# Inverse softmax sums carried to the attention outputs: through DRAM as rows instead of widened copies and TensorE transposes

## The chip, the cores and the metric

The kernel runs on one core of a Trainium2 chip. Its time is the device time of one execution in microseconds (us). Before the change it is 1243.0 us, the median of three runs (1238.74, 1243.0 and 1247.97).

The core has five instruction streams that run beside each other, each in its own order: TensorE (PE, whose weight loads are shown as PEld), VectorE (DVE), ScalarE (ACT), GpSimd (POOL) and the queue that issues the DMAs (SP). Semaphores tie them together.

## The reference

A forgetting attention over 8 batches of 8 heads (576 positions, 64 numbers each), and behind it a feed-forward network over all 4608 tokens, in float32:

```python
scores = scale * np.matmul(q, k.transpose(0, 1, 3, 2))
decay = cum[:, :, :, None] - cum[:, :, None, :]      # cum: running sum of log f
scores = np.where(causal, -1000000000.0, scores + decay)
scores = scores - np.max(scores, axis=-1, keepdims=True)
attn = np.exp(scores)
attn = attn / (np.sum(attn, axis=-1, keepdims=True) + 1e-09)
x = np.matmul(attn, v)                               # heads side by side: 4608 x 512
h = x @ w_in                                         # 512 -> 2048
out = np.maximum(0.01 * h, h) @ w_out                # 2048 -> 512
```

## The kernel before

Every large product is made of three products of rounded parts (`_h` is the high part of a number, `_l` the low part), which is why the feed-forward network, lines L508 and L541, has most of TensorE's matmuls.

**Stages.** First an early stage (to about 160 us): the first 256 positions of batches 0, 1 and 2, and the splitting of the weights. Then 64 tasks, one for each head, in the order of `ORDER` (batches 0, 3, 4, 5, 6, 7, 1, 2). A head of batches 0 to 2 has three chunks of positions left (2, 3 and 4: 320 positions, the last chunk 64 wide), a head of the others five (0 to 4: 576 positions). Last comes what is left of the feed-forward network.

**One iteration** `t` of the loop over tasks works on two heads at once: for each chunk `i` it transposes the probabilities of head `t - 1` (`transposes`, PSUM tiles `tr`, copied out by ACT as `ph` and by DVE as `pl`), and computes the scores of head `t` (`scores`, PSUM tiles `sc`, a masked minimum on DVE, and the exponential on ACT, which also adds up the row sums into `fixed["sum.."]`). Then it computes the outputs of head `t - 1` (`values`, PSUM tiles `av`). Between these pieces `fill(step)` puts portions of the feed-forward network: `h_` tiles (L508), and `o_` tiles (L541), which need `gh` (DVE, L518) and `gl` (POOL, L520).

**Where the sums go.** The outputs of two heads share one tile `x`, with positions as columns and the two heads' 64 numbers as partitions (0 to 63 and 64 to 127). The sums have positions as partitions: `fixed["sum.."]` is 128 x 5 chunks x 2 heads. Once for each pair of heads, in the iteration behind the second head, `inverse` takes the reciprocal (L440, L441) and has POOL repeat each value 64 times into `rw` (L448). `normalise` transposes `rw` on TensorE chunk by chunk into the PSUM tile `rb` (L459), so that each position's factor stands in its column on all 64 partitions of its head; DVE multiplies `x` with it (L460), and the product goes to `xd` in DRAM (L464), from where the feed-forward network fetches it as `xs` (L475).

**What sets the order.** The program is written with a framework that reorders each engine's instructions by its own estimates and gives out buffers by tag. The PSUM tag `tr` has two buffers, which `tr`, `av` and `rb` share, so a tile waits until the last but one before it has been read. The SBUF tags `part0` and `part1`, which hold `rw`, have one buffer each. All DMAs are issued by SP, one after the other: an issue that waits holds up all behind it.

Of the kernel before, what the change touches and what calls it, by code (L numbers as in the profile page):

```python
# [8 lines left out]
F32 = mybir.dt.float32  # L9
# [4 lines left out]
ALU = mybir.AluOpType  # L14

P = 128
# [20 lines left out]
def forgetting_attention_ffn(ctx, tc, qT, kT, v4, vr, f, w_in, w_out, out):  # L37
# [6 lines left out]
    nc = tc.nc  # L44
    NHEAD, D, S = qT.shape
# [4 lines left out]
    NFULL = S // P  # L50
    REST = S - NFULL * P
    NCH = NFULL + 1
# [11 lines left out]
    tasks = [  # L64
        (b * HPB + x, T // P if b < NE else 0, NCH) for b in batches for x in range(HPB)
    ]

    def rows(i):
        return P if i < NFULL else REST

    def width(i):
        return i * P + rows(i)
# [18 lines left out]
    one = ctx.enter_context(tc.tile_pool(name="one", bufs=1))  # L91
    dram = ctx.enter_context(tc.tile_pool(name="dram", bufs=1, space=bass.MemoryType.DRAM))
    psum = ctx.enter_context(tc.tile_pool(name="psum", bufs=2, space=bass.MemoryType.PSUM))
# [18 lines left out]
    ident = ident_r.bitcast(F32)  # L112
# [6 lines left out]
    )  # L119

    xd = dram.tile([DM, NTOK], F32, name="xd")
    dec_k, dec_q = (dram.tile([NHEAD, 2, S], F32, name=n) for n in ("dec_k", "dec_q"))

    fr = one.tile([2 * NHEAD, S], F32, tag="z4", name="fr")
# [59 lines left out]
    for i, r in enumerate(decay_r):  # L184
        n = width(i)
        d = one.tile([P, n], F32, tag=f"z{i}", name=f"d_{i}")
# [4 lines left out]
    for i in range(NCH):  # L191
        c = slice(i * P, width(i))
# [3 lines left out]
    for name, tag, x, to in (("fck", "s1", fc, dec_k), ("fcq", "m1", start, dec_q)):  # L196
        r = one.tile([P, S], F32R, tag=tag, name=name, bufs=2)
# [5 lines left out]
    pairs = {}  # L203

    def load(t):

        s, c0, c1 = tasks[t]
        h = state[t] = {}
        a, n = c0 * P, width(c1 - 1)
        for name, src, lo in (("q", qT, a), ("k", kT, 0)):  # L210
            x = h[name] = one.tile([P, S], F32, tag=f"{name}raw", name=f"{name}raw_{t}")
            for o in range(2):
                nc.sync.dma_start(x[o * D:(o + 1) * D, lo:n], src[s][:, lo:n])
        if s % 2 == 0:
            g = s // 2
            vm = fixed["vm"]
            nc.sync.dma_start(vm[:, :, :NFULL], v4[g])
            nc.sync.dma_start(vm[:REST, :, NFULL], vr[g])
            pairs[s // 2, c0] = {}
# [79 lines left out]
    fixed = {}  # L299
# [38 lines left out]
    def scores(t, i):  # L338

        s, c0, c1 = tasks[t]  # L340
        h = state[t]
        m, n = rows(i), width(i)
        if i < NFULL:
            z = h[f"z{i}"] = one.tile([P, n], F32, tag=f"z{i}", name=f"z{i}_{t}")
        else:
            z = h[f"z{i}"] = fixed["z4"]
        z = z[:m, :n]
        if i == c0:
            h["max"] = one.tile([P, NCH + 1], F32, tag="max", name=f"max_{t}", bufs=3)
        parts = [(0, n)] if n <= 512 else [(0, n // 2), (n // 2, n)]  # L350
        for x, (a, b) in enumerate(parts):
            ps = psum.tile([P, 512], F32, tag="sc", name=f"sc_{t}_{i}_{x}")
            cols = slice(i * P, i * P + m)
            for y, w in enumerate("12"):
                nc.tensor.matmul(  # L355
                    ps[:m, :b - a], h["s" + w][:, cols], h["m" + w][:, a:b],
                    start=y == 0, stop=y == 1,
                )
            at = TRI - P - i * P + a
            nc.vector.tensor_tensor_reduce(  # L360
                out=z[:, a:b], in0=ps[:m, :b - a], in1=tri[:m, at:at + b - a], scale=-SCALE,
                scalar=3.0e38 if x == 0 else h["max"][:m, i:i + 1],
                op0=ALU.add, op1=ALU.min, accum_out=h["max"][:m, i + x:i + x + 1],
            )
        last = i + len(parts) - 1
        nc.scalar.activation(  # L366
            z, z, AF.Exp, bias=h["max"][:m, last:last + 1], scale=-1.0,
            accum_out=fixed["sum" + "ab"[s // 2 % 2]][:m, i, s % 2:s % 2 + 1],
        )

    def transposes(t, i):
        h = state[t]
        if i == tasks[t][1]:
            for w in ("ph", "pl"):
                h[w] = one.tile([P, PTW], F32R, tag=w, name=f"{w}_{t}")
        m = rows(i)
        z = h[f"z{i}"]
        ps = psum.tile([P, 512], F32, tag="tr", name=f"tr_{t}_{i}")

        blocks_ = [NFULL, *range(NFULL)] if i == NFULL else range(i + 1)  # L380
        for x, j in enumerate(blocks_):
            nc.tensor.transpose(  # L382
                ps[:, x * m:(x + 1) * m], z[:m, j * P:(j + 1) * P], ident[:m, :m]
            )
        nblk = len(blocks_)
        for dst, eng in ((h["ph"], "a"), (h["pl"], "v")):
            if nblk == 1:
                o, hi, src = dst[:, PT0:], h["ph"][:, PT0:], ps[:, :m]
            else:
                first = 0 if i == NFULL else place_p(0, i * P)  # L390
                o = strided(dst, first, nblk, PST, m)
                hi = strided(h["ph"], first, nblk, PST, m)
                src = ps[:, :nblk * m].rearrange("p (j m) -> p j m", m=m)
            if eng == "a":
                nc.scalar.copy(o, src)  # L395
            else:
                nc.vector.tensor_tensor(o, src, hi.bitcast(F32), op=ALU.subtract)  # L397
# [37 lines left out]

    def inverse(t):

        s, c0, c1 = tasks[t]
        r = one.tile([P, NCH, 2], F32, tag="r", name=f"r_{t}")
        nc.vector.tensor_scalar(r, fixed["sum" + "ab"[s // 2 % 2]], 1.0e-9, None, op0=ALU.add)  # L440
        nc.vector.reciprocal(r, r)  # L441
        wide = pairs[s // 2, c0]["r"] = {}
        for lo, hi in spans(t):
            c = (hi - lo + P - 1) // P
            w = one.tile([P, c, 2, D], F32, tag=f"part{lo == 0:d}", name=f"rw_{t}_{lo}")
            a = r[:, lo // P:lo // P + c]
            a = bass.AP(tensor=a.tensor, offset=a.offset, ap=[*a.ap, [0, D]])
            nc.gpsimd.tensor_copy(w, a)  # L448
            wide[lo] = w.rearrange("p c o d -> p c (o d)")

    def normalise(t):

        s, c0, c1 = tasks[t]
        pair = pairs[s // 2, c0]
        x, r = pair["x"], pair["r"]
        for part, (lo, hi) in enumerate(spans(t)):
            ps = psum.tile([P, 512], F32, tag="tr", name=f"rb_{t}_{part}")
            for c in range(lo, hi, P):
                nc.tensor.transpose(ps[:, c - lo:c - lo + P], r[lo][:, (c - lo) // P], ident)  # L459
            nc.vector.tensor_tensor(x[:, lo:hi], x[:, lo:hi], ps[:, :hi - lo], op=ALU.mult)  # L460
        b, hp = s // HPB, (s % HPB) // 2
        a, n = c0 * P, width(c1 - 1)
        at = place[b, a]
        nc.sync.dma_start(xd[hp * P:(hp + 1) * P, at:at + n - a], x[:, a:n])  # L464

    def spans(t):
        a, n = tasks[t][1] * P, width(tasks[t][2] - 1)
        return [(a, n)] if n - a <= 512 else [(a + P, n), (a, a + P)]
# [96 lines left out]
    def fill(n):  # L565

        credit[0] += n
        while credit[0] >= 1:
            credit[0] -= 1
            if not next(quanta, None):  # L570
                credit[0] = 0
                return
            used[0] += 1
# [32 lines left out]
    for t in range(nt + 1):  # L606
        heads[0] = t < nt
        if t + 1 < nt:
            load(t + 1)
        before = list(range(*tasks[t - 1][1:])) if t else []  # L610
        now = list(range(*tasks[t][1:])) if t < nt else []
        have = ready[0] // T * NQ - used[0]
        left = min((e + 2 - t for e in ends if e + 1 >= t), default=1)
        step = min(have / (left + SLACK), MAXQ) / 8
        fill(step)
        for i in range(5):
            if i in before:
                transposes(t - 1, i)
            if i in now:
                scores(t, i)  # L620
            fill(step)
        if t:
            for part in range(len(spans(t - 1))):
                if part == 0 and tasks[t - 1][0] % 2:
                    inverse(t - 1)
                values(t - 1, part)
                fill(step)
            if tasks[t - 1][0] % 2:
                normalise(t - 1)
            s, c0, c1 = tasks[t - 1]  # L630
            if s % HPB == HPB - 1:
                ready[0] = place[s // HPB, c0 * P] + width(c1 - 1) - c0 * P
        if t + 1 < nt:
            split(t + 1)
        fill(step * (3 - len(spans(t - 1)) if t else 1))
# [35 lines left out]
```

## Time and profile before

| | |
|---|---|
| median of three runs | 1243.0 us |
| the profiled execution | 1237.03 us, of it 1235.3 us from the first to the last instruction |
| PE busy | 1219.8 us (99%) |
| PEld, ACT, DVE, POOL busy | 1077.1, 635.2, 609.6, 444.0 us |
| granted TensorE clock | 1.00 |
| DMA | 102.47 MB, 27.3% of the 16 engines' span |

Busy time is the time in which an engine had an instruction of the program under way. PE's matmuls overlap each other, so the sum of their durations is more than the busy time, and what one of them costs is better read from the distance between ends. In the profile's rows `out<-in` are tiles by the program's names; a row of the grouped view has the count behind an x, the busy time in us, the mean duration in ns, and the engine's idle time just before these instructions with what ended it. In rows in order of time the first two numbers are the start and the time taken, in us.

### The profile page before, as it was taken

Reading aid. Unit: us, or ns where it says so; the run is one execution under the profiler, and the core shown is the slowest. Engines: PE = TensorE matmul, PEld = TensorE weight load, DVE = VectorE, ACT = ScalarE, POOL = GpSimd, SP = SyncE. Lnnn points to the kernel's source line nnn. Section 1 sums busy time; section 2 is a strip of 40 time slices with the busy share of each in tenths; the row PEclk is TensorE's granted clock in tenths of the full one; section 3 lists DMA queues with packets and bytes.
Section 4 is the critical chain, followed back from the end, with each engine's and each line's share of the span. In section 5 each row is a group of like instructions: output and inputs, shape, how many; then the busy total and the mean of one; then the engine's idle time right before and its main releaser. Section 6 shows DMA issues by size and latency. Waiting matters only on the chain.

```text
span 1235.3 us, 21918 instructions
## 1 busy us (share of the span) xinstructions
PE 1219.8 (99%) x7980; PEld 1077.1 (87%) x7980; DVE 609.6 (49%) x1598; ACT 635.2 (51%) x1511; POOL 444.0 (36%) x395
## 2 busy tenths in 40 slices
PE   9999999999999999999999999999999999999998
PEld 6777788888888989899899999999999998889997
DVE  6888975665554444444434434344343334443211
ACT  6775646667755565555544545454444444651111
POOL 2000254555444344543444443443344334432000
PEclk9999999999999999999999999999999999999999
DMA  6453433343232223322221222221222222211000
GB/s 195 149 168 134 140 100 101 91 119 111 80 113 67 69 84 86 99 69 86 78 86 49 79 69 80 66 77 46 74 73 68 64 61 80 57 53 40 18 18 18
DMA packets 70219, 102.47 MB, mean 83 GB/s; under 512 B 13152, under 2 KB 42384, under 8 KB 70112
## 3 DMA queue, kind: packets, MB, share of 16 engines
q1 hardware_dynamic: 70112, 101.08, 27.3%
q8 instruction: 63, 1.03, 0.4%
q14 instruction: 44, 0.36, 0.1%
HBM read 74.76 MB, written 18.42 MB: 75 GB/s over the span
## 4 chain that ended last, share of the span: by engine, by line
PE 84%; DMA 5%; issue 3%; DVE 3%; ACT 2%; POOL 2%; SPq 1%; POOLq 0%; ACTq 0%; DVEq 0%
PE h L508 29%; PE o L541 29%; PE sc L355 8%; PE av L424 7%; PE tr L382 6%; DMA xs<-xd 2%; PE sce L246 1%; PE rb L459 1%; PE ave L288 1%; DMA xd<-x 1%; DMA kraw<-in_kT 1%; PE sce L249 1%; ACT wt L150 1%; PE warm L105 1%; POOL s L129 1%
## 5 line engine op out<-in xcount | busy, mean ns | idle before, releaser
L508 PE MATMUL h<-xh,win_h 128*128 128x256 f32 x1152 | 331.2, 288 | 0.1
L508 PE MATMUL h<-xh,win_l 128*128 128x256 f32 x1152 | 326.0, 283 | 0.0
L508 PE MATMUL h<-xs,win_h 128*128 128x256 f32 x1024 | 289.2, 282 | 0.0
L520 POOL TENSOR_TENSOR gl<-g,gh 128x512 fp32r<-128x512 f32 x111 | 143.0, 1289 | 307.8 <-DVE gh L518 307.7
L541 PE MATMUL o<-wout_h,gh 128*128 128x512 f32 x576 | 231.0, 402 | 1.5 <-DVE gh L518 1.5
L541 PE MATMUL o<-wout_l,gh 128*128 128x512 f32 x576 | 226.0, 393 | 0.1
L541 PE MATMUL o<-wout_h,gl 128*128 128x512 f32 x576 | 224.8, 392 | 0.7 <-DVE gl L520 0.7
L508 PEld LDWEIGHTS h<-xh,win_h 128*128 128x128 f32 x1152 | 219.4, 191 | 4.4 <-ACT win_h L155 0.5
L508 PEld LDWEIGHTS h<-xh,win_l 128*128 128x128 f32 x1152 | 219.5, 190 | 0.9 <-issue 0.7
L515 ACT ACTIVATE g<-h 128x512 f32<-128x512 f32 x144 | 85.9, 597 | 229.2 <-PE h L508 220.8
L508 PEld LDWEIGHTS h<-xs,win_h 128*128 128x128 f32 x1024 | 195.1, 191 | 3.0
L395 ACT CAST ph<-tr 128x256 fp32r<-128x256 f32 (+3 forms) x272 | 119.5, 445 | 143.2 <-PE tr L382 141.8
L360 DVE CUSTOM_DVE_ANT_0 z<-sc,tri 128x128 f32<-128x128 f32 (+1 forms) x208 | 107.4, 518 | 166.1 <-PE sc L355 166.1
L518 DVE CAST gh<-g 128x512 fp32r<-128x512 f32 x144 | 76.6, 532 | 181.8 <-ACT g L515 179.0
L366 ACT ACTIVATE z<-z,max 128x128 f32<-128x128 f32 (+1 forms) x208 | 122.7, 590 | 79.8 <-DVE max L360 78.7
L397 DVE TENSOR_TENSOR pl<-tr,ph 128x256 fp32r<-128x256 f32 (+3 forms) x272 | 136.7, 508 | 41.4 <-ACT ph L395 41.2
L129 POOL TENSOR_TENSOR s<-qraw,s 64x576 fp32r<-64x576 f32 (+1 forms) x64 | 79.4, 1240 | 182.2 <-ACT s L326 164.5
L541 PEld LDWEIGHTS o<-wout_h,gl 128*128 128x128 f32 x576 | 108.1, 188 | 24.7 <-DVE gl L520 1.2
L355 PE MATMUL sc<-m,s 128*64 128x288 f32 (+1 forms) x336 | 123.2, 372 | 1.8 <-DVE max L360 1.8
L541 PEld LDWEIGHTS o<-wout_h,gh 128*128 128x128 f32 x576 | 108.4, 189 | 18.0 <-DVE gh L518 1.7
L541 PEld LDWEIGHTS o<-wout_l,gh 128*128 128x128 f32 x576 | 108.5, 189 | 16.3 <-issue 0.3
L382 PE MATMUL tr<-ident_r,z 128*128 128x128 f32 x568 | 96.1, 273 | 1.7 <-DVE pl L397 1.1
(112 smaller groups left out, 1807.8 us busy)
## 6 DMA issues: line engine op xcount, KB each, us to landing
kraw<-in_kT SPq DMA_DIRECT2D x128, 144.0 KB
qraw<-in_qT SPq DMA_DIRECT2D x80, 144.0 KB
wraw<-in_w_in SPq DMA_DIRECT2D x16, 512.0 KB
wraw<-in_w_out SPq DMA_DIRECT2D x16, 512.0 KB
fixed_vm<-in_v SPq DMA_DIRECT2D x32, 256.0 KB
xs<-xd SPq DMA_DIRECT2D x16, 512.0 KB
out<-ost SPq DMA_DIRECT2D x28, 256.0 KB
xd<-x SPq DMA_DIRECT2D x20, 288.0 KB
```

The lines of the kernel that those rows point to most:

```text
L129: nc.gpsimd.tensor_tensor(out, a, b, op=ALU.subtract)
L355: nc.tensor.matmul(ps[:m, :b - a], h["s" + w][:, cols], h["m" + w][:, a:b], start=y == 0, stop=y == 1,)
L360: nc.vector.tensor_tensor_reduce(out=z[:, a:b], in0=ps[:m, :b - a], in1=tri[:m, at:at + b - a], scale=-SCALE, scalar=3.0e38 if x == 0 else ...
L366: nc.scalar.activation(z, z, AF.Exp, bias=h["max"][:m, last:last + 1], scale=-1.0, accum_out=fixed["sum" + "ab"[s // 2 % 2]][:m, i, s % 2: ...
L382: nc.tensor.transpose(ps[:, x * m:(x + 1) * m], z[:m, j * P:(j + 1) * P], ident[:m, :m])
L395: nc.scalar.copy(o, src)
L397: nc.vector.tensor_tensor(o, src, hi.bitcast(F32), op=ALU.subtract)
L424: nc.tensor.matmul(ps[:, a - lo:hi - lo], fixed["vs"][:, odd, j, :], h[w][:, at:at + hi - a], start=(n == 0), stop=(n == len(steps) - 1),)
L508: nc.tensor.matmul(ph[:, e, :], w[:, c, fs], xx[:, c, :], start=(c == 0 and x == 0), stop=(c == NCC - 1 and x == 2),)
L515: nc.scalar.activation(g, ph, AF.Prelu, alpha=0.01)
L520: eng.tensor_tensor(gl, g, gh.bitcast(F32), op=ALU.subtract)
L541: nc.tensor.matmul(acc[k], gg[:, e, ts], w[:, e, :], start=(fc_ == 2 * p0 and x == 0), stop=(fc_ == 2 * p1 - 1 and x == 2),)
```

## The change

`inverse` no longer widens on POOL. The reciprocals are laid out with the two heads outermost (10 columns), transposed by one TensorE instruction into 10 rows of 128, copied out by ACT into the unused half of the tile `rest`, and written to a small DRAM tile by one DMA. Four DMAs read them back, each value row repeated over the 64 partitions of its head: two into `main` (the full chunks) and two into `rest` (the last 64 positions). `normalise` loses its transposes; DVE multiplies `x` with `main` and `rest`, which lie in SBUF. The call of `inverse` moves from ahead of `values` to behind chunk 1 of the same iteration.

```diff
+    rows_d = [dram.tile([2, NCH * P], F32, name=f"rows_{x}") for x in range(4)]
...
     def inverse(t):
         s, c0, c1 = tasks[t]
-        r = one.tile([P, NCH, 2], F32, tag="r", name=f"r_{t}")
-        nc.vector.tensor_scalar(r, fixed["sum" + "ab"[s // 2 % 2]], 1.0e-9, None, op0=ALU.add)
+        r = one.tile([P, 2, NCH], F32, tag="r", name=f"r_{t}")
+        sums = fixed["sum" + "ab"[s // 2 % 2]].rearrange("p c o -> p o c")
+        nc.vector.tensor_scalar(r, sums, 1.0e-9, None, op0=ALU.add)
         nc.vector.reciprocal(r, r)
-        wide = pairs[s // 2, c0]["r"] = {}
-        for lo, hi in spans(t):
-            c = (hi - lo + P - 1) // P
-            w = one.tile([P, c, 2, D], F32, tag=f"part{lo == 0:d}", name=f"rw_{t}_{lo}")
-            a = r[:, lo // P:lo // P + c]
-            a = bass.AP(tensor=a.tensor, offset=a.offset, ap=[*a.ap, [0, D]])
-            nc.gpsimd.tensor_copy(w, a)
-            wide[lo] = w.rearrange("p c o d -> p c (o d)")
+        ps = psum.tile([P, 512], F32, tag="tr", name=f"rt_{t}")
+        nc.tensor.transpose(ps[:2 * NCH, :P], r.rearrange("p o c -> p (o c)"), ident)
+        main = one.tile([P, NFULL * P], F32, tag="part0", name=f"rb_{t}")
+        rest = one.tile([P, 2 * P], F32, tag="part1", name=f"rbr_{t}")
+        flat = rest[:2 * NCH, P:]
+        nc.scalar.copy(flat, ps[:2 * NCH, :P])
+        to = rows_d[s // 2 % 4]
+        nc.sync.dma_start(to.rearrange("o (c q) -> (o c) q", q=P), flat)
+        for y, lo, hi in ((main[:, c0 * P:], c0 * P, NFULL * P), (rest[:, :REST], NFULL * P, S)):
+            for o in range(2):
+                nc.sync.dma_start(
+                    y[o * D:(o + 1) * D], to[o:o + 1, lo:hi].broadcast_to([D, hi - lo])
+                )
+        pairs[s // 2, c0]["r"] = main, rest
     def normalise(t):
...
-        for part, (lo, hi) in enumerate(spans(t)):
-            ps = psum.tile([P, 512], F32, tag="tr", name=f"rb_{t}_{part}")
-            for c in range(lo, hi, P):
-                nc.tensor.transpose(ps[:, c - lo:c - lo + P], r[lo][:, (c - lo) // P], ident)
-            nc.vector.tensor_tensor(x[:, lo:hi], x[:, lo:hi], ps[:, :hi - lo], op=ALU.mult)
+        for y, lo, hi in ((main[:, c0 * P:], c0 * P, NFULL * P), (rest[:, :REST], NFULL * P, S)):
+            nc.vector.tensor_tensor(x[:, lo:hi], x[:, lo:hi], y, op=ALU.mult)
...
             if i in now:
                 scores(t, i)
+            if i == 1 and t and tasks[t - 1][0] % 2:
+                inverse(t - 1)
             fill(step)
...
-                if part == 0 and tasks[t - 1][0] % 2:
-                    inverse(t - 1)
                 values(t - 1, part)
```

How the instructions stand now is read from the built programs; the changed program's line numbers are higher by one above `inverse` and by six at the end, and the last number in a name only tells tiles apart. TensorE first, at the pair of heads 18 and 19, the sixth pair with all five chunks (about 393 us). Before, chunk 1 of head 19 is transposed (`tr_1`), chunk 1 of head 20 scored (`sc_1`), and chunk 2 follows at once:

```order
L382 MATMUL tr_1_4717<-ident_r,z_19_4532 128x128 x2
L355 MATMUL sc_1_0_4723<-m_20_4663,s_20_4662 128x256
L355 MATMUL sc_1_0_4723<-fixed_m2a,fixed_s2a 128x256
L382 MATMUL tr_2_4728<-ident_r,z_19_4562 128x128 x3
L355 MATMUL sc_2_0_4735<-m_20_4663,s_20_4662 128x384
L355 MATMUL sc_2_0_4735<-fixed_m2a,fixed_s2a 128x384
```

Now the transpose of the inverses (`rt`) stands there:

```order
L383 MATMUL tr_1_4736<-ident_r,z_19_4551 128x128
L356 MATMUL sc_1_0_4742<-m_20_4682,s_20_4681 128x256
L356 MATMUL sc_1_0_4742<-fixed_m2a,fixed_s2a 128x256
L446 MATMUL rt_4750<-ident_r,r_4747 10x128
L356 MATMUL sc_2_0_4767<-m_20_4682,s_20_4681 128x384
L356 MATMUL sc_2_0_4767<-fixed_m2a,fixed_s2a 128x384
L514 MATMUL h_4_4723<-xh_4300,win_h_97 128x256
L383 MATMUL tr_2_4760<-ident_r,z_19_4581 128x128
```

`tr_2` has moved behind the scores and one feed-forward matmul, because it now gets the PSUM buffer that `rt` leaves. The five transposes of this pair at its end, `L459 MATMUL rb_0_4840<-ident_r,rw_128_4803 128x128 x4` and one more for `rb_1`, are gone.

SP at the same pair, behind the loads of the head after the next one. Before:

```order
L213 DMA qraw_4879<-in_qT 64x576 x2
L213 DMA kraw_4882<-in_kT 64x576 x2
L329 DMA fixed_s2a<-dec_q 2x576
L328 DMA fixed_s2a<-s_22_5029 64x576
L330 DMA fixed_m2a<-dec_k 2x576
```

and now:

```order
L214 DMA qraw_4897<-in_qT 64x576 x2
L214 DMA kraw_4900<-in_kT 64x576 x2
L452 DMA rows_127<-rbr_4753 10x128
L455 DMA rb_4752<-rows_127 64x512 x2
L455 DMA rbr_4753<-rows_127 64x64 x2
L330 DMA fixed_s2a<-dec_q 2x576
L329 DMA fixed_s2a<-s_22_5047 64x576
L331 DMA fixed_m2a<-dec_k 2x576
```

So the write of the rows and the four reads stand between the loads and the three DMAs with which head 22's operands (`s2`, `m2`) are put together.

DVE at the end of the same pair: `x` gets its sums (L433, before L432), and is then multiplied by `rest` and `main`.

```order
L433 TENSOR_TENSOR x_4642<-av_0_4832,y_0_4843 64x448
L466 TENSOR_TENSOR x_4642<-x_4642,rbr_4753 128x64
L433 TENSOR_TENSOR x_4642<-av_1_4859,y_1_4862 64x128
L466 TENSOR_TENSOR x_4642<-x_4642,rb_4752 128x512
L524 CAST gh_5_4893<-g_5_4891 128x512
```

Before, the two multiplications stood together behind the second sum, and read PSUM (`rb_0` for 448 columns, `rb_1` for 128). The reciprocals stand where they stood on DVE, at the end of the iteration before, as soon as the last sums are there.

More of the change, by code (lines that the diff above doesn't have):

```diff
@@ L454, in normalise @@
         pair = pairs[s // 2, c0]
-        x, r = pair["x"], pair["r"]
-        for part, (lo, hi) in enumerate(spans(t)):
-            ps = psum.tile([P, 512], F32, tag="tr", name=f"rb_{t}_{part}")
-            for c in range(lo, hi, P):
-                nc.tensor.transpose(ps[:, c - lo:c - lo + P], r[lo][:, (c - lo) // P], ident)
-            nc.vector.tensor_tensor(x[:, lo:hi], x[:, lo:hi], ps[:, :hi - lo], op=ALU.mult)
+        x, (main, rest) = pair["x"], pair["r"]
+        for y, lo, hi in ((main[:, c0 * P:], c0 * P, NFULL * P), (rest[:, :REST], NFULL * P, S)):
+            nc.vector.tensor_tensor(x[:, lo:hi], x[:, lo:hi], y, op=ALU.mult)
         b, hp = s // HPB, (s % HPB) // 2
```

## The prediction

> **What bounds the kernel now.** I read the shares of busy time first, then the slices, then the chain of work that ended last.
>
> ```profile
> PE 1219.8 (99%) x7980; PEld 1077.1 (87%) x7980; DVE 609.6 (49%) x1598; ACT 635.2 (51%) x1511; POOL 444.0 (36%) x395
> PEclk9999999999999999999999999999999999999999
> PE 84%; DMA 5%; issue 3%; DVE 3%; ACT 2%; POOL 2%; SPq 1%; POOLq 0%; ACTq 0%; DVEq 0%
> 160.00:262.00 102.00, 101.35 (x681) 89.89 (x680) 62.12 (x162) 63.57 (x150) 53.40 (x46) 1.00 0.35 100
> 262.00:360.00 98.00, 96.83 (x656) 85.54 (x655) 56.08 (x179) 65.33 (x173) 48.55 (x44) 1.00 0.37 105
> 360.00:960.00 600.00, 597.86 (x4012) 541.52 (x4012) 262.10 (x769) 308.57 (x746) 255.62 (x218) 1.00 0.25 74
> 960.00:1126.00 166.00, 165.82 (x1120) 149.12 (x1119) 67.98 (x188) 80.26 (x179) 62.67 (x58) 1.00 0.20 56
> ```
>
> The last four rows are stretches of the tasks (length; busy time of PE, PEld, DVE, ACT and POOL; clock; share and rate of DMA). From 160 us to 1126 us PE is without work for 966.0 - 961.9 = 4.1 us in all, at full clock. DVE, ACT and POOL have 40 to 60% left. So where the change acts, **TensorE's own instructions set the time**: what is taken from its stream comes off the end, as long as nothing new makes it wait. DVE and POOL work counts only through such a wait.
>
> **What the change takes from TensorE.**
>
> ```profile
> 597.78 0.39 PE L541 MATMUL o<-wout_l,gh 128*128 128x512 f32 x1
> 598.00 0.40 PE L541 MATMUL o<-wout_h,gl 128*128 128x512 f32 x1
> 598.24 0.71 PE L459 MATMUL rb<-ident_r,rw 128*128 128x128 f32 x5
> 598.70 0.48 PE L541 MATMUL o<-wout_h,gh 128*128 128x512 f32 x1
> L459 PE MATMUL rb<-ident_r,rw x136: 270/272/331, 188.2 to 1123.3; 128*128 128x128 f32 x136
>   DVE x L432: 1.6, 6
>   issue: 0.4, 2
>   POOL fixed_m2a L129: 0.3, 1
> ```
>
> A transpose lasts 272 ns, but they overlap. The `o` matmul ahead of the five ends at 598.40, the one behind at 599.18: 0.78 us between ends. Without transposes two `o` matmuls follow each other at 0.23 us (597.78 and 598.00 are 0.22 apart). So five transposes take 0.55 us of TensorE, 0.11 us each, and 136 of them (12 pairs with 3, 20 pairs with 5) take 15.0 us. Under the line's own rows stands what PE and PEld waited ahead of them: 1.6 + 0.4 + 0.3 = 2.3 us, mostly for DVE to read a `tr` buffer. Sum taken away: **17.3 us**.
>
> **What it adds to TensorE.** One transpose for each pair, 32 in all. Its stationary operand is 10 columns wide instead of 128, and the identity still streams 128 columns. The trace has no such shape. Between nothing and 0.27 us (the whole duration of an `rb`) I take the streamed width, as in the row above, 0.11 us: **3.5 us**, between 0 and 8.6.
>
> **Waits around the new transpose.** `rt` needs the reciprocals and a `tr` buffer, and its own buffer comes free when ACT has copied it. The prices are read at heads 18 and 19, and at heads 12 and 13:
>
> ```profile
> 393.51 0.49 PE L382 MATMUL tr<-ident_r,z 128*128 128x128 f32 x3
> 394.04 0.48 ACT L395 CAST ph<-tr 128x384 fp32r<-128x384 f32 x1 [0.19 <-PE tr L382]
> L431 ACT COPY y<-av 64x128 f32<-64x128 f32 x40 | 10.4, 261 | 30.9 <-PE av L424 18.9 <-DVE x L432 11.6
> 304.16 0.22 DVE L441 RECIPROCAL r<-r 128x10 f32<-128x10 f32 x1
> 307.77 0.62 DVE L397 TENSOR_TENSOR pl<-tr,ph 128x128 fp32r<-128x128 f32 x2
> 307.99 0.40 PE L541 MATMUL o<-wout_h,gh 128*128 128x512 f32 x1
> 308.00 0.21 ACT L366 ACTIVATION_READ_ACCUMULATOR z<-z,max 128x1 f32 x1
> 308.76 0.51 ACT L366 ACTIVATE z<-z,max 128x256 f32<-128x256 f32 x1 [0.54 <-DVE max L360]
> ```
>
> The reciprocals end at 304.38 and `rt` stands at 307.99 (just ahead of that `o` matmul), so they are not waited for. At heads 18 and 19, `rt` starts at 393.51 in place of `tr_2`, ends at 393.8, and ACT, which had 0.19 us free ahead of 394.04, copies it in 0.26 us (the row of 128 columns) to about 394.15. PE reaches `tr_2` after two score matmuls and one `h`, about 0.6 us behind `rt`, and waits 0.2 us; the pair of heads 26 and 27 has the same order. In the other pairs with this hand-over of the buffer six or more feed-forward matmuls lie between, over 1 us, which hide the copy. In the first four pairs with five chunks `rt` waits instead for DVE to read `tr_0`: at heads 12 and 13 the two reads begin at 307.77 and take 0.62 us together, so the first ends at about 308.08, 0.1 us behind the place of `rt`; I take 0.15 us each. I take 2 x 0.2 + 4 x 0.15 + 0.2 for the rest = **1.2 us**. On ACT the 32 copies cost 32 x 0.26 = 8 us, most of it in idle time (at 308.21 ACT is free until 308.76), but in a few pairs the copy goes ahead of a `ph` cast that PE needs soon: another **0.5 us**, between 0 and 3.
>
> **The round trip through DRAM.** This is the added wait. Behind the DVE multiplication stand the `gh` casts and the score minima of the next head, so a late DMA would stop DVE and then PE. One of the tightest pairs, heads 12 and 13, again:
>
> ```profile
> 306.02 0.59 SPq L213 DMA_DIRECT2D kraw<-in_kT  x1
> 312.98 0.23 SPq L329 DMA_DIRECT2D fixed_s2a<-dec_q  x1
> 316.45 0.29 DVE L432 TENSOR_TENSOR x<-av,y 64x128 f32<-64x128 f32 x1 [0.32 <-ACT y L431]
> 316.94 0.82 DVE L460 TENSOR_TENSOR x<-x,rb 128x448 f32<-128x448 f32 x2 [0.19 <-PE rb L459]
> 468.15 0.54 SPq L464 DMA_DIRECT2D xd<-x  x1
> 471.36 0.39 SPq L475 DMA_DIRECT2D xs<-xd  x1
> 474.91 0.69 DVE L480 CAST xh<-xs 128x1024 fp32r<-128x1024 f32 x1 [1.74 <-DMA xs<-xd]
> 252.06 5.34 DMA kraw<-in_kT
> 179.23 0.22 DVE L441 RECIPROCAL r<-r 128x10 f32<-128x10 f32 x1
> 188.70 0.49 DVE L460 TENSOR_TENSOR x<-x,rb 128x320 f32<-128x320 f32 x1 [0.41 <-PE rb L459]
> 1113.66 0.22 DVE L441 RECIPROCAL r<-r 128x10 f32<-128x10 f32 x1
> 1124.28 0.49 DVE L460 TENSOR_TENSOR x<-x,rb 128x320 f32<-128x320 f32 x1
> ```
>
> `rt` runs from about 308.1 to 308.45, and ACT's copy ends at about 308.75. SP has nothing to do from 306.61 to 312.98. The trace has one round trip of the same kind: `xd` written, then read as `xs`. From the issue of the write to the issue of the read, which waits for it, 3.21 us; from the issue of the read of 512 KB to the cast that waited for it, 3.55 us. For `main` a second issue of 0.6 us comes between, so it lands at most 3.2 + 0.6 + 3.55 = 7.4 us after 308.85, at 316.25; it is needed at 316.74, when the last sum ends. The small `rest`, issued two places later, is needed first, at 316.13: 308.85 + 3.2 + 1.8 leaves it 2.3 us to land. The bytes are fewer than in the rows (5 KB written, 256 KB read), so I take 6 us for the trip, which leaves about 1.5 us. Below, nothing excludes 4 us; above, the chain has one load that took 5.34 us to land, which with 3.2 + 0.6 makes 9.2 us. From the reciprocals to the multiplication the first and the last of the 32 pairs have 9.3 and 10.4 us (the last four rows), and the first eight and last four all 9 to 13; less what lies ahead of the copy, 1 to 4.5 us, this leaves about 7 to 9 us for the trip in these 12. In the 20 between it is 16.7 us and more, and at least 9 for the trip. **Cost taken: nothing**, hidden by the transposes, scores and outputs of the same iteration. SP is held until about 308.85 + 3.2 + 2.4 = 314.4 instead of 312.98, so the head after the next gets its operands up to 1.5 us later, with a whole iteration in between.
>
> **DVE and POOL.**
>
> ```profile
> L448 POOL COPY rw<-r x52: 287/504/690, 179.6 to 1114.0; 128x512 f32<-128x512 f32 x20, 128x128 f32<-128x128 f32 x20, 128x384 f32<-128x384 f32 x12
> L440 DVE TENSOR_SCALAR r<-fixed_suma x16: 173/816/1415, 178.4 to 1091.6; 128x10 f32<-128x10 f32 x16
> 361.64 2.40 POOL L129 TENSOR_TENSOR xs<-xs,xh 128x1024 fp32r<-128x1024 f32 x1 [3.75 <-DVE xh L480]
> L518 DVE CAST gh<-g 128x512 fp32r<-128x512 f32 x144 | 76.6, 532 | 181.8 <-ACT g L515 179.0 <-issue 0.4 <-PE o L541 0.2
> 361.82 2.50 DVE L518 CAST gh<-g 128x512 fp32r<-128x512 f32 x1
> ```
>
> POOL loses 52 copies of 0.5 us, 25 us off the bound. DVE keeps the same number of columns in 64 multiplications, now with both inputs in SBUF. That can cost: an addition on 10 columns, SBUF to SBUF, takes 173 ns at best and 816 ns in the middle, and a cast that takes 0.53 us on average took 2.50 us beside a POOL operation of 2.40 us. So DVE operations on SBUF queue behind POOL's. If each multiplication loses the same 0.6 us, it is 38 us of DVE time. The 40 multiplications of the 20 pairs in the middle have cover (DVE is busy 262 of 600 us there); for the other 24 I take no cost to TensorE either, and leave it to a rival.
>
> [...]
>
> **The sum.** 17.3 - 3.5 - 1.2 - 0.5 = 12.1 us. The profiled execution took 1237.0 us (a span of 1235.3 and 1.7 around it), so the changed one would take 1225. That execution lies 6 us under the median of the runs shown; against the median, 1243.0 - 12.1 = **1231 us**.
>
> **Rivals.**
>
> 1. [...] In the 12 tight pairs DVE is busy about 60% of the time and follows PE closely. Two multiplications with 0.6 us each make 12 x 2 x 0.6 = 14 us; if half reaches PE through late `gh`, `pl` and minima, 7 us of the gain go: 1238 us. For it: the 816 ns above. Against it: today DVE waits for `rb` there (0.19 us in the row of 316.94), which ends.
> 2. *The round trip is late* (the slower side). If 64 reads of the same row take as long as the worst load, with the fourth issue in the way, the trip is 3.2 + 1.8 + 5.34 = 10.3 us, against 8 us: 2.3 us late in each of 12 pairs, 28 us on DVE and behind it on PE. 1231 + 28 = 1259 us. It decides from about 9 us on, where 12 x 1 us eat the gain. Against it: the 3.55 us above for twice the bytes.
> 3. *More than the transposes comes back.* If `rt`, with 10 columns to load, costs half, and the waits of 1.7 us don't appear, 17.3 - 1.8 = 15.5 us; with POOL's and DVE's earlier `gl` and `gh` up to 2 us more: 1226 us.
> 4. *The change doesn't do what it says*: the order of instructions shows the transposes and copies gone and nothing else moved far, so I give it no chance.
>
> **How the numbers follow.** Chances: the sum as it stands 0.60 (1226 to 1236), rival 1 0.20, rival 3 0.13, rival 2 0.07. The range from 1223 to 1244 leaves out rival 2 and a little at both ends; it holds the spread of the runs (4 to 5 us either side) and the bounds of `rt`. A change of 1%, 12.4 us, is about what a measurement of this kernel can tell from no change, and the sum lies at that edge: of the 0.60, 0.29 go to faster and 0.31 to the same. Faster 0.29 + 0.13 = 0.42, the same 0.31 + 0.20 = 0.51, slower 0.07.
>
> **What would show it.** [...] The prediction is wrong if PE's waits, now 4.1 us in the tasks, grow by more than 2 us.

## The result, and the profile after

The changed kernel takes **1235.1 us** (median of 14 runs, 1229.2 to 1244.9), beside 1243.0 us for the kernel before (14 runs, 1235.8 to 1248.0). The ratio is 0.9948, with a 95% interval from 0.9924 to 0.9972: about 6 us less, where the forecast had 12.1 us less. One run of the kernel before, of 2480.7 us, is in no figure below.

The profiled executions show why both kernels spread over 10 us. Every run lists the mean clock that TensorE was granted, and the time follows it: the kernel before took 1235.7 us at a clock of 1.000 and 1249.7 us at 0.988. Over 233 runs of 12 kernels (with an offset for each kernel and chip) 0.001 of clock is 1.08 us, and what is left scatters by 1.0 us. So beside each ratio I give the time **at full clock**: a run's time less 1.08 us for each 0.001 that its clock is under 1.000, the mean over the runs, and the difference to the kernel before on the same chip in the same comparison (± is a 95% interval, from that scatter and the number of runs). That tells 1 us apart where the ratio tells 4. Run again on one chip with the kernel before, the changed kernel stands at 1228.1 us, **8.1 us (± 0.7) under the kernel before**, 1236.2. This figure takes out falls of the clock inside the tasks too, which the last section comes to. The profiled execution took 1233.0 us (a span of 1230.9) at a clock of 0.995; that of before had 1.000.

From its page: busy times, the granted clock in 40 slices, and the chain of work that ended last. Then the stretches of the tasks, with the same columns as before.

```profile
PE 1211.4 (98%) x7876; PEld 1067.3 (87%) x7876; DVE 638.2 (52%) x1610; ACT 643.3 (52%) x1543; POOL 431.4 (35%) x343
PEclk9899999999999999999999999999999999999999
PE 87%; DMA 4%; DVE 3%; ACT 3%; issue 1%; SPq 1%; POOL 1%; ACTq 0%; POOLq 0%; DVEq 0%
```

```profile
160.00:262.00 102.00, 101.25 (x672) 89.15 (x670) 64.25 (x162) 63.22 (x149) 50.67 (x41) 1.00 0.38 107
262.00:360.00 98.00, 96.03 (x650) 84.62 (x650) 61.52 (x185) 69.44 (x182) 47.65 (x37) 1.00 0.41 117
360.00:960.00 600.00, 595.80 (x3973) 538.88 (x3973) 281.75 (x773) 312.53 (x766) 250.21 (x186) 1.00 0.28 83
960.00:1126.00 166.00, 164.94 (x1106) 147.90 (x1105) 71.94 (x193) 80.79 (x184) 60.94 (x51) 1.00 0.23 66
```

TensorE still sets the time, but in the tasks it is now without work for 966.0 - 958.0 = 8.0 us instead of 4.1. DVE is 28.6 us busier, although its multiplications have the same columns. The second slice of the clock (8; from 30 to 62 us the mean is 0.89, before 1.00) lies ahead of the tasks, in a stage that the change doesn't touch. What TensorE waited for from 160 to 1126 us, the changed kernel first, the kernel before second (engine, line and tile, what it waited for: us in total, times, longest):

```profile
PE tr L383 <- DVE pl L398: 3.2, 2, 2.3
PE tr L383 <- DVE x L433: 1.7, 1, 1.7
PE sc L356 <- DVE max L361: 1.7, 2, 1.1
PE rt L446 <- DVE r L444: 0.6, 1, 0.6
PE av L425 <- ACT ph L396: 0.3, 1, 0.3
PE rt L446 <- DVE pl L398: 0.2, 1, 0.2
```

```profile
PE sc L355 <- DVE max L360: 1.8, 3, 1.0
PE tr L382 <- DVE pl L397: 1.1, 1, 1.1
PE tr L382 <- DVE x L432: 0.5, 1, 0.5
PE rb L459 <- DVE x L432: 0.4, 2, 0.2
```

7.7 us against 3.8, and nearly all of it for DVE: TensorE arrives at the same places earlier, and DVE's results don't come earlier by as much, or come later. The experiments ask why DVE is late.

### The profile page after: what moved, and what is told of

Read it like the earlier page. It is cut to its first block, busy times and chain, and to the rows that moved or that the text cites. A ratio compares the mean times of both kernels' runs of the same rounds, so it can differ in the third digit from the quotient of the medians.

```text
span 1230.9 us, 21897 instructions
## 1 busy us (share of the span) xinstructions
PE 1211.4 (98%) x7876; PEld 1067.3 (87%) x7876; DVE 638.2 (52%) x1610; ACT 643.3 (52%) x1543; POOL 431.4 (35%) x343
## 4 chain that ended last, share of the span: by engine, by line
PE 87%; DMA 4%; DVE 3%; ACT 3%; issue 1%; SPq 1%; POOL 1%; ACTq 0%; POOLq 0%; DVEq 0%
PE h L514 30%; PE o L547 29%; PE sc L356 8%; PE av L425 8%; PE tr L383 7%; DMA xs<-xd 2%; PE sce L247 1%; PE ave L289 1%; DMA xd<-x 1%; PE sce L250 1%; PE warm L105 1%; ACT wt L151 1%; PE tre L280 1%; DMA wraw<-in_w_in 0%; DVE gh L524 0%
```

## The experiments

Every theory speaks of these 4 us. **Theory A**: five more DMAs in SP's queue make the loads and the fetches late. **Theory B**: the multiplications, now with two inputs in SBUF, queue behind POOL's operations. **A third** came up with the results: places where loads were only just in time before. In all variants of the changed kernel TensorE's instructions stand in the same order as in the changed kernel; where the other engines' order moved in a way that counts, it is said.

| kernel | ratio to before, 95% interval | at full clock | against before on the same chip |
|---|---|---|---|
| changed, again | 0.9935 (0.9906 to 0.9963) | 1228.1 | -8.1 ± 0.7 |
| without the DMAs | 0.9943 (0.9912 to 0.9974) | 1226.7 | -9.5 ± 0.7 |
| without the multiplications | 0.9894 (0.9858 to 0.9930) | 1224.7 | -11.5 ± 0.9 |
| without both | 0.9924 (0.9894 to 0.9954) | 1224.0 | -11.6 ± 0.7 |
| multiplications with an input in PSUM | 0.9940 (0.9910 to 0.9969) | 1226.1 | -9.6 ± 0.7 |
| multiplications on POOL | 0.9956 (0.9930 to 0.9982) | 1228.7 | -6.9 ± 0.7 |
| before, without the multiplications | 1.0009 (0.9982 to 1.0036) | 1234.8 | -0.8 ± 0.7 |
| two reads for four | 1.0006 (0.9981 to 1.0031) | 1234.7 | -1.5 ± 0.7 |
| each read twice | 0.9993 (0.9964 to 1.0023) | 1234.4 | -1.5 ± 0.8 |
| one read for each head, pairs of three chunks | 0.9891 (0.9852 to 0.9929) | 1226.3 | -9.6 ± 1.0 |
| the same again | 0.9915 (0.9882 to 0.9947) | 1226.3 | -10.3 ± 0.9 |
| one read for each head, all pairs | 0.9923 (0.9894 to 0.9951) | 1226.4 | -10.2 ± 0.8 |

**The changed kernel again.** No edit.

> The changed kernel once more, unaltered. In the first pair of profiles it started the tasks 1.84 us later than before (first reciprocal at 181.29 us instead of 179.44) in a stage that the change does not touch, and TensorE was without work for 8.0 us in the tasks instead of 4.1. If the 1.84 us were chance, the first reciprocal stands again at 179.4 to 180 here, and the time is 10 us under before in the profiles; if they belong to the change, it stands at 181.3 again. The waits in the tasks, if they come from the order of the program (both theories below), come back at the same places: 1.7 us ahead of a transpose of heads 8 and 9, 2.2 us near 366 us, 1 us near 1039 us, and 7 to 9 us in all. Time: 1233 to 1236, 7 to 10 us under before.

The first reciprocal ended at 184.6 us, later still, with a clock of 0.96 in the first 160 us; in other kernels of this series with a clock of 1.00 there it ended at 179. The first profile of the changed kernel has 0.98 there, so its 1.84 us go with the clock, not with the change. The waits came back at their places: 1.8 us for `x`, 3.7 for `pl`, 1.2 for the minima, 0.9 at `rt`, 7.6 us in all. They belong to the program.

**Without the DMAs** (the copy's target becomes a small tile of its own).

```
-        nc.sync.dma_start(to.rearrange("o (c q) -> (o c) q", q=P), flat)
...
-                nc.sync.dma_start(
-                    y[o * D:(o + 1) * D], to[o:o + 1, lo:hi].broadcast_to([D, hi - lo])
-                )
...
-            nc.vector.tensor_tensor(x[:, lo:hi], x[:, lo:hi], y, op=ALU.mult)
+            nc.vector.tensor_tensor(x[:, lo:hi], x[:, lo:hi], tri[:, :hi - lo], op=ALU.add)
```

> The DMA that writes the rows and the four that read them back are left out; DVE adds a constant tile of zeros instead of multiplying (two inputs in SBUF as before, same columns), so the output is not normalised. The new transpose and ACT's copy stay. Theory A (SP's queue: the loads, xd and xs stand behind five more DMAs, of which the second waits for the first to land): kraw, qraw and xs land as early as before, TensorE's waits in the tasks fall from 8.0 us to about 4.5 and the time by 3.5 us, to 1231.5. Theory B (DVE's two-SBUF-input operations queue behind POOL's): they take the same 477 and 777 ns in the middle, the waits stay at about 8 us and the time at 1235.

1.4 us (± 1.0) came back, less than half of what theory A asked for. TensorE's waits fell to 5.3 us: those at `rt`, one at `av` and most of those for the minima went, but the largest, for `x` at heads 8 and 9, grew to 2.6 us. That one needs no new DMAs.

**Without the multiplications.**

```
-        x, (main, rest) = pair["x"], pair["r"]
-        for y, lo, hi in ((main[:, c0 * P:], c0 * P, NFULL * P), (rest[:, :REST], NFULL * P, S)):
-            nc.vector.tensor_tensor(x[:, lo:hi], x[:, lo:hi], y, op=ALU.mult)
+        x = pair["x"]
```

> The 64 multiplications are left out (the output is not normalised); transposes, copies and all five DMAs of each pair stay. Theory A: SP's queue is as long as in the changed kernel, kraw and qraw are as late, TensorE's waits in the tasks stay at 7 to 8 us (xd is ready up to 1.3 us earlier, which may save 1 us of them), the time stays at 1234 to 1235. Theory B: DVE is 40 us less busy, gh, pl and the score minima come earlier, the waits fall to 4.5 us or under, and the time to 1231 or under.

3.4 us (± 1.1) came back, as theory B has it; the waits fell to 4.7 us. But an engine that does less is also less in the way, whether POOL holds it up or not: the next two runs part these.

**Multiplications with an input in PSUM.**

```
+        pair["ps"] = ps
...
-            nc.vector.tensor_tensor(x[:, lo:hi], x[:, lo:hi], y, op=ALU.mult)
+            k = max((hi - lo) // P, 1)
+            a = ps[:, :(hi - lo) // k]
+            a = bass.AP(tensor=a.tensor, offset=a.offset, ap=[a.ap[0], [0, k], a.ap[1]])
+            xx = x[:, lo:hi].rearrange("p (k m) -> p k m", k=k)
+            nc.vector.tensor_tensor(xx, xx, a, op=ALU.mult)
```

> The multiplications of the changed kernel take their second input from PSUM (the sums of the last product, as many columns; not the inverse row sums) instead of the SBUF tiles, all DMAs stay. Theory lock (two SBUF inputs queue behind POOL's operations): the 64-column multiplications fall from 477 ns in the middle to about 0.25 us, those of 512 from about 1.0 to 0.7 us, and at full clock the time falls from 1228.1 to about 1225.5. Theory own time (any multiplication at this place costs that much): 1228.

The groups of DVE by shape (count, busy us, mean ns of one, idle before), the changed kernel's first:

```profile
L466 DVE TENSOR_TENSOR x<-x,rb 128x512 f32<-128x512 f32 x20 | 24.6, 1232 | 0.7
L466 DVE TENSOR_TENSOR x<-x,rbr 128x64 f32<-128x64 f32 x32 | 18.2, 569 | 0.7
L466 DVE TENSOR_TENSOR x<-x,rb 128x256 f32<-128x256 f32 x12 | 6.3, 529 | 0.4
```

```profile
L471 DVE TENSOR_TENSOR x<-x,av 128x512 f32<-128x512 f32 x20 | 13.8, 689 | 0.7
L471 DVE TENSOR_TENSOR x<-x,av 128x64 f32<-128x64 f32 x32 | 6.8, 214 | 0.0
L471 DVE TENSOR_TENSOR x<-x,av 128x256 f32<-128x256 f32 x12 | 5.1, 421 | 0.4
```

49.1 us against 25.7: the second SBUF input costs DVE 23.4 us, and the mean of 64 columns falls from 569 to 214 ns. (In this version both multiplications of a pair also stand behind the second sum, since they need the last product.) Where it comes about can be read in the changed kernel's own rows at heads 12 and 13 (POOL first, then DVE: start, duration):

```profile
317.69 1.45 POOL L130 TENSOR_TENSOR fixed_m2a<-kraw,m 64x576 fp32r<-64x576 f32 x1
319.21 0.88 POOL L130 TENSOR_TENSOR fixed_vs<-fixed_vm,fixed_vs 128x320 fp32r<-128x320 f32 x1
```

```profile
318.75 0.47 DVE L466 TENSOR_TENSOR x<-x,rbr 128x64 f32<-128x64 f32 x1
319.58 1.06 DVE L466 TENSOR_TENSOR x<-x,rb 128x512 f32<-128x512 f32 x1
```

The first begins while POOL is at work, and ends at 319.22, 0.08 us behind POOL's 319.14. The second begins in POOL's next operation, which ends at 320.09, and itself ends 0.55 us later. With an input in PSUM 64 columns take 0.21 us and 512 take 0.69, so by that measure the first did 0.13 us of its work in its 0.39 us beside POOL, and the second 0.14 in its 0.51: by these rows both stood still for most of the time until POOL had finished. "Lock" in the expectations is a name for this; what holds DVE up, no run shows. TensorE feels only part of it: the time falls by 1.5 us (± 1.0).

Where it reaches TensorE can be followed at heads 8 and 9. The product of the pair before goes out as `xd`, the fetch of `xs` is issued behind it, and DVE's `xh` cast waits for the fetch. Behind the cast stand the score minimum, the exponentials, the reciprocals and the sum `x`. The times are us from the start of the first reciprocal in the same profile:

| | before | changed | again | no DMAs | no multiplications | input in PSUM |
|---|---|---|---|---|---|---|
| `xd` issued | 68.76 | 70.34 | 70.33 | 69.56 | 67.81 | 68.76 |
| `xs` issued | 71.70 | 72.76 | 72.76 | 71.92 | 71.34 | 71.72 |
| `xh` cast starts | 77.37 | 78.55 | 78.85 | 78.91 | 77.26 | 77.09 |
| TensorE's wait for `x` | 0.49 | 1.70 | 1.78 | 2.59 | 1.11 | 0.59 |

With all DMAs in place, the multiplication with an input in PSUM brings `xd` and the cast back to where they were. Without the DMAs `xs` is issued earlier too, but the cast is as late as in the changed kernel: the fetch takes longer there, which no run explains.

**Before, without the multiplications.**

```
-            nc.vector.tensor_tensor(x[:, lo:hi], x[:, lo:hi], ps[:, :hi - lo], op=ALU.mult)
```

> The kernel before without its multiplications (its transposes and copies stay; no normalisation). Theory lock: an unlocked multiplication costs TensorE little, the time falls by 1 us or less, from 1236.1 to about 1235.5 at full clock, so that of the 3.5 us of the changed kernel 2.5 or more are the lock. Theory own time: it falls by about 3 us, to 1233.

0.8 us (± 0.7): with an input in PSUM the multiplications were nearly hidden in the kernel before. In the changed kernel they cost 3.4 (± 1.1), of which 1.5 (± 1.0) go when one input comes from PSUM.

**Without both.**

```
-        nc.sync.dma_start(to.rearrange("o (c q) -> (o c) q", q=P), flat)
...
-                nc.sync.dma_start(
-                    y[o * D:(o + 1) * D], to[o:o + 1, lo:hi].broadcast_to([D, hi - lo])
-                )
...
-            nc.vector.tensor_tensor(x[:, lo:hi], x[:, lo:hi], y, op=ALU.mult)
```

> Both are left out of the changed kernel: the five DMAs of each pair and the 64 multiplications (no normalisation). At full clock the kernel before stands at 1236.1 us, the changed one at 1228.1, the one without the DMAs at 1226.6, without the multiplications at 1224.6. If the two costs add up, 1.5 and 3.5 us, this one stands at 1223.1, 13.0 under before, and the forecast sum of 12.1 is all there. If they hide each other, or a third cause (loads and scores that were only just in time before) takes a share, it stands at 1224 to 1225.

-11.6 us, 0.1 us under the kernel without multiplications (± 1.1, on another chip). Once the multiplications are gone, the DMAs cost nothing that can be told. Added up, the two costs would have given -12.9; that they overlap is likely, but 1.3 us is no more than the error of such a sum. And not all is back: against the kernel before *without its multiplications* on the same chip this is 10.8 us (± 0.9), not 12.1. What TensorE waits for here:

```profile
PE tr L383 <- DVE x L433: 1.9, 1, 1.9
PE tr L383 <- DVE pl L398: 1.6, 1, 1.6
PE sc L356 <- DVE max L361: 0.2, 1, 0.2
```

In the kernel before without multiplications the same two waits are 0.4 and 1.0 us. At heads 8 and 9 DVE's `xh` cast waits 2.2 us for the fetch of `xs`. It starts 77.4 us behind the first reciprocal, as in the kernel before, but takes 1.49 us beside a POOL operation (257.94 to 259.36) where it took 0.69. Near 366 us it waits 2.5 us, and behind it stands the `gh` cast, which beside POOL's `xs` took 2.47 us in the changed kernel (POOL 2.36) and 2.50 in the kernel before (POOL 2.40). That these are the causes is read from the rows; no run took them away.

**The multiplications on POOL.**

```
-            nc.vector.tensor_tensor(x[:, lo:hi], x[:, lo:hi], y, op=ALU.mult)
+            nc.gpsimd.tensor_tensor(x[:, lo:hi], x[:, lo:hi], y, op=ALU.mult)
```

> The 64 multiplications run on POOL instead of DVE. DVE is about 46 us less busy, POOL about 50 to 60 us more (1.29 us for 512 columns by its gl row). If POOL's idle time takes them, the time is near that without multiplications, 1225 to 1226 at full clock. Rival: gl, xs and the lower halves of q and k queue behind them on POOL and TensorE waits, 1230 or more.

Neither number came: 1228.7, nothing gained; set against the kernel before, each on its chip, it is 1.2 us (± 1.0) behind the changed kernel. 512 columns take POOL 1.29 us. TensorE waited 2.3 us for `x`, 2.3 at one `rt`, 2.0 for `pl` and 1.3 for a minimum.

**Two reads for four.**

```
-            for o in range(2):
-                nc.sync.dma_start(
-                    y[o * D:(o + 1) * D], to[o:o + 1, lo:hi].broadcast_to([D, hi - lo])
-                )
+            a = to[:, lo:hi]
+            a = bass.AP(tensor=a.tensor, offset=a.offset, ap=[a.ap[0], [0, D], a.ap[1]])
+            nc.sync.dma_start(y, a)
```

> The four reads of a pair become two: one DMA for both heads' 64 partitions each, for main and for rest. Same bytes. SP issues 64 DMAs less, and by the rows of the four reads (about 0.5 us each, 2.4 us from the first to the last at 244 us) is free about 1 us earlier in each pair. Theory A: the stall of 1.7 us of heads 8 and 9 falls to about 0.7, TensorE's waits in the tasks fall from 8.0 to about 6 us, and the time by 2 us, to 1233. Theory B: no change, 8 us and 1235.

Neither theory had this: 6.6 us **slower** than the changed kernel with fewer DMAs and the same bytes. Here the prediction's rival 2, the late round trip, came about. DVE's waits, then its row at heads 12 and 13:

```profile
DVE x L465 <- DMA rbr<-rows: 13.3, 9, 3.6
```

```profile
322.78 0.23 DVE L465 TENSOR_TENSOR x<-x,rbr 128x64 f32<-128x64 f32 x1 [3.57 <-DMA rbr<-rows]
```

The busy share of the 16 DMA engines in tenths and the GB/s, in 40 slices from 311 to 319 us, the changed kernel first (reads issued at 312.27 to 314.64), then this one (314.10 and 314.68):

```profile
DMA  0002100000005297785321110000000599700003
GB/s 0 0 0 82 26 0 0 0 0 0 0 0 51 20 205 184 256 277 184 110 64 27 33 24 21 18 0 0 0 0 0 150 219 207 184 23 0 0 0 69
```

```profile
DMA  0000300000000000000000111111111111111111
GB/s 12 0 0 0 82 0 23 0 0 3 0 0 0 0 0 0 0 0 0 0 0 0 31 51 41 61 41 61 41 61 41 61 41 61 41 61 41 61 41 61
```

With the four reads the engines reach a digit of 9 (90% or more), at 184 to 277 GB/s for a microsecond. With the two reads, whose source has 2 rows outermost, they stay at a digit of 1, which stands for 10 to 20%, at about 50 GB/s, and DVE gets the last of them 8.1 us after its issue (314.68 to 322.78). Why they are slower, no run shows. In part the 6.6 us are another thing: at one place (640.1 us) DVE's order changed and the `xh` cast stands ahead of a score minimum, where TensorE waited 3.5 us.

**Each read twice.**

```
-            for o in range(2):
+            for o in (0, 1, 0, 1):
```

> Each of the four reads of a pair is issued twice, into the same tile (eight reads instead of four; a second read may also wait for the first one of its tile). SP is held 2.4 us longer or more for each pair, and the tiles are ready that much later. If the reads and SP's place in the program are hidden but for what the kernel without DMAs showed (1.5 us at full clock), the second four add about as much again: 1230 at full clock instead of 1228.1. If the trip was only just in time (7 to 9 us of cover in the first eight pairs and the last four), the multiplications now wait for the reads in these 12 pairs, 1 to 3 us each, and the time is 1236 to 1250.

6.6 us (± 1.0) slower than the changed kernel, between the two expectations. DVE now waits for the reads:

```profile
DVE x L466 <- DMA rb<-rows: 10.2, 7, 3.3
DVE x L466 <- DMA rbr<-rows: 4.1, 6, 1.2
```

TensorE's waits rise to 14.7 us. Not all of it need be the reads: the order moved too, in five of the first eight pairs (the 64-column multiplication stands later on DVE) and at six heads (the cast of `kraw` on ACT). So the round trip of the changed kernel is hidden, but with little to spare; a few microseconds more, and rival 2 would have been the result.

**One read for each head.** Pairs of three chunks have 320 columns, so that `main` holds them all: `blocks_of` gives one block there, and the two blocks as before in the other pairs.

```
+        if S - a <= NFULL * P:
+            return [(main[:, :S - a], a, S)]
+        return [(main[:, a:], a, NFULL * P), (rest[:, :REST], NFULL * P, S)]
```

> In the 12 pairs with three chunks (320 columns) main and rest become one tile: one read for each head instead of two, each still of 64 partitions, and one multiplication instead of two. The 20 other pairs are as in the changed kernel. SP issues 24 DMAs less and DVE 12 multiplications less (477 ns in the middle). Of 64 multiplications 12 go, of the lock's 2.1 us about 0.4, of the trip's 1.5 us at most 24/160, 0.2: 1227.5 at full clock, 0.6 under the changed kernel. If the reads behaved as the pair of 128-partition reads did, the time would be above 1228.

> The version with one read for each head in the pairs of three chunks once more, on one chip with the version for all pairs: 1226.2 at full clock, 2 us under the changed kernel. If the 2 us were chance, it stands at 1227.5 to 1228.

Each time 1226.3 us at full clock, 1.8 us (± 1.0) under the changed kernel and 9.6 and 10.3 under before: half the reads and half the multiplications of the 12 tight pairs are gone, and each read still fills 64 partitions from one row. I had reckoned 0.6 us. That the pairs without cover are the ones that pay fits the next run, but it isn't shown more directly.

**One read for each head in all pairs** (a tile of 576 columns, in the space of two early partial outputs).

```
+        nc.vector.tensor_tensor(x[:, c0 * P:S], x[:, c0 * P:S], wide[:, c0 * P:S], op=ALU.mult)
```

> One read for each head and one multiplication in all 32 pairs: the tile for the inverse sums has 576 columns and more in the space of the two early partial outputs, which become halves of one tile. SP issues three DMAs in each pair instead of five, DVE 32 multiplications instead of 64. In the 20 pairs in the middle DVE and SP have cover, so at full clock at most 0.5 us under the version with one read only in the pairs of three chunks (1226.2): 1225.7 to 1226.5. If the multiplication of the 64 last columns now starts later, since it waits for the second sum, and xd and xs come later, it is above 1227.

1226.4: no more, as expected if the 20 pairs in the middle have cover. The version for the pairs of three chunks beats both kernels.

## Why the prediction was right or wrong

The forecast was 1231 us and the main case 1226 to 1236; 1235.1 lies in it, at its slow end. At equal clock the gain was 8.1 us (± 0.7) where the sum had 12.1. By its steps:

- **What bounds.** Right. With the order of TensorE kept, every microsecond found came from its stream, its waits or its clock.
- **136 transposes at 0.11 us, 15.0 us, and 32 `rt` at 0.11, 3.5 us.** Right. `rt` between a score matmul and an output matmul:

```profile
585.15 0.28 PE L356 MATMUL sc<-fixed_m2a,fixed_s2a 128*128 128x256 f32 x1
585.27 0.27 PE L446 MATMUL rt<-ident_r,r 128*10 128x128 f32 x1
585.30 0.48 PE L547 MATMUL o<-wout_h,gh 128*128 128x512 f32 x1
```

  The end of `rt` lies 0.11 us behind that of the score matmul, and the next one's 0.24 behind its own. Over all matmuls, the median distance between ends of each line and shape times its count sums to 1172.7 us before and 1161.1 after: 11.6 us less, where 15.0 - 3.5 is 11.5.
- **Waits of 2.3 us that go with the old transposes.** Right. From the end of the matmul ahead of a group of `rb` to the end of the one behind it, less the usual distance of that one, the 136 take 17.4 us in the profile of before; the prediction had 17.3.
- **Waits round `rt` 1.2 us, ACT's copy 0.5 us.** About right: measured in the same way the 32 `rt` take 5.3 us, 1.8 over 3.5, TensorE's wait at `av` is 0.3, and the copies cost ACT what the row for 128 columns gave:

```profile
L446 PE MATMUL rt<-ident_r,r x32: 269/271/276, 181.6 to 1113.3; 128*10 128x128 f32 x32
L450 ACT COPY rbr<-rt x32: 238/254/256, 181.9 to 1113.7; 10x128 f32<-10x128 f32 x32
```

  So where the instructions changed, TensorE is 17.4 - 5.3 = 12.1 us better off, as the sum has it. What is missing lies elsewhere: its waits ahead of all other instructions grew from 3.4 to 6.9 us.
- **The earlier call of `inverse`.** Nothing by itself: made alone in the kernel before, it leaves every engine's order in the built program as it was.
- **The round trip costs nothing, hidden.** Right for the wait that I priced: no multiplication of the changed kernel waits for a DMA.
- **SP held up to 1.5 us longer, "with a whole iteration in between".** The hold was right, its price of nothing wasn't. At heads 8 and 9 the four reads of the pair before keep SP until 246.40, and counted from the first reciprocal the loads of `kraw` are issued 1.1 us later than before. In all pairs together the DMAs cost 1.4 us (± 1.0), and nothing that can be told once the multiplications are gone. The largest wait, that for `x` at heads 8 and 9, isn't due to them, as the table above shows; those at `rt`, at `av` and for the minima went or shrank with them.
- **The multiplications cost TensorE nothing.** This step failed, and it is the largest term. The queueing behind POOL was there, though smaller on DVE than forecast (38 us; 23.4 measured), and rival 1 priced it at 7 us at TensorE; measured are 1.5 us (± 1.0) for the second input in SBUF and 3.4 (± 1.1) for the multiplications as a whole, against 0.8 (± 0.7) in the kernel before. One way to TensorE was overlooked: the product leaves for DRAM later, and the fetch behind it too. The rows at heads 8 and 9 of the kernel before, then of the changed one (1.8 us of each difference arise ahead of the tasks, at a clock of 0.98 beside 1.00):

```profile
247.99 0.35 SPq L464 DMA_DIRECT2D xd<-x  x1
250.93 0.54 SPq L475 DMA_DIRECT2D xs<-xd  x1
256.59 0.69 DVE L480 CAST xh<-xs 128x1024 fp32r<-128x1024 f32 x1 [1.53 <-DMA xs<-xd]
```

```profile
251.41 0.35 SPq L470 DMA_DIRECT2D xd<-x  x1
253.83 0.54 SPq L481 DMA_DIRECT2D xs<-xd  x1
259.62 0.90 DVE L486 CAST xh<-xs 128x1024 fp32r<-128x1024 f32 x1 [2.27 <-DMA xs<-xd]
```

  The prediction also called DVE about 60% busy in all 12 tight pairs; in the last four it was 41% (68.0 of 166 us).
- **What is late next.** Not asked at heads 8 and 9 and near 366 us, where TensorE already waited 0.5 and 1.1 us for DVE: by then some microseconds of its work had been taken away, and these waits were bound to grow. Without DMAs and multiplications they are 1.9 and 1.6 us. That is enough for the 1.3 us (± 0.9) between 12.1 and the 10.8 of the like comparison.
- **"Wrong if PE's waits grow by more than 2 us."** They grew from 4.1 to 8.0, so by its own sign the prediction was wrong in this step. That 1235.1 still lies in the main case is in part luck: the range of 5 us either side was taken for the spread of the runs, and it covered a loss of 4 us that the sum had put at nothing.

## What to carry to other kernels

Work taken from the bounding engine comes back only as far as the next engine's results were early: list the places where the bound engine already waits a little, since the gain is lost there first. Price each DMA that is added also by what stands behind it in its queue, and each operation that loses its PSUM operand by what runs on POOL beside it (here 64 columns took 569 ns instead of 214), and by the transfers that stand behind its result. With broadcast DMAs it matters which are merged: here the merge over the two heads cost 6.6 us (in part by a changed order), while the merge along the columns, with half the multiplications, gained 1.8 us (± 1.0) in the pairs of three chunks and no more in the others. Merge first in the stages without cover.

## What the runs showed of the hardware

- The granted clock explains nearly all of the spread: 1.08 us for each 0.001, with 1.0 us left over. Differences of 1 to 2 us that the ratios (± 0.3%) do not show can be told with it, but not all of the clock is chance.
- In the changed kernel's profile the clock is 0.50 inside the tasks once, from 366.3 to 369.7 us, behind a TensorE wait of 2.3 us that ends at 365.7; behind its wait of 1.7 us, which ends at 263.8, the clock stays at 1.00. In the profile of before no wait in the tasks is longer than 1.1 us, and the clock is 1.00 throughout. That is the order of events; no run tried whether the wait brings the fall. In the fall `h` matmuls start 0.21 us apart, and 0.12 behind it, so the 3.4 us lose about 1.5 us (an estimate from these distances), and the time at full clock leaves this out: from the start of the first reciprocal to that of the last the changed kernel's two profiles take 6.1 and 6.2 us less than that of before (934.4, 928.3, 928.2). For the first of the two, with the 1.5 and the last pair's transposes, which lie behind that, this is about the 8.1. None of the changed kernel's 26 runs has a mean clock of 1.000; of the 95 runs of the kernel before that stand beside the variants, 22 have.
- At heads 12 and 13 the two reads of 128 partitions each (2 rows outermost in the source) kept the 16 DMA engines 10 to 20% busy at about 50 GB/s; the same bytes in four reads of 64 partitions moved at 184 to 277 GB/s.
- A write of 5 KB to DRAM holds the read that waits for it on SP only shortly: 30.5 us for 31 pairs in the changed kernel, 1.0 us each (3.0 at most). From the issue of the write to that of the first read it is 1.5 us in the mean, where the prediction took 3.2 from `xd` and `xs`.

```profile
SPq L455 <- DMA rows<-rbr: 30.5, 31, 3.0
```
